# Moving one input load to another queue, and the output weights behind four small copies, in a fused Mamba-2 and bilinear FFN kernel

## The chip, the cores and the metric

The kernel runs on one core of one Trainium2 chip. The metric is device time in microseconds (us) of one execution, and of several executions the median. Engines are named as in the profile: PE (TensorE, matmuls; PEld is its weight load), DVE (VectorE), ACT (ScalarE), POOL (GpSimd) and SP (SyncE, which here only issues DMAs). ACT and POOL issue DMAs too.

## What is computed

The input is a state-space layer with decay, in chunks, followed by a bilinear feed-forward layer. x is (4, 8, 768, 32), a (4, 8, 768), B and C (4, 8, 768, 16); the weights w_a and w_b are 256 x 1536 and w_out is 1536 x 256. Cut to what matters:

```
cum = cumsum(log(a))                      # inside a chunk
M = (C @ B.T) * exp(cum_i - cum_j), j <= i
y = M @ x + exp(cum) * (C @ state)
state = exp(sum(log a)) * state + sum_j B_j x_j exp(cum_last - cum_j)
x2 = y, heads side by side                # (3072, 256)
out = ((x2 @ w_a) * (x2 @ w_b)) @ w_out   # (3072, 256), f32
```

The result does not depend on the chunk length. The kernel works with blocks of 128 tokens.

## The kernel before

**Tiling.** 768 tokens make six blocks of 128. Four batch elements make two pairs per block, so there are twelve "pairs": pairs 0 and 1 are block 0, pairs 2 and 3 block 1, and so on. For a block, products of decays (`scan`, L248, into `Pr`) are turned into factors per token. B is divided by them and C multiplied (`scale_bc`, L324, tiles `bm` and `cm` for pairs 0 and 1; `scale_q`, L341, into `planes` for later blocks), both are transposed, and PE forms scores C B^T (`scores`, L398) in four PSUM banks `SC`. `mask` (L442) multiplies the scores with a causal table, on DVE straight from PSUM or on POOL after an ACT copy. PE multiplies the masked scores with x (`pv_u`, `pv1`, `pv_b`), and the state is carried from block to block. The result, in f16, is the moving operand of the feed-forward matmuls: `unit_mm` and `bunit` multiply with `Wa` and `Wb`, ACT copies the first product out of PSUM, DVE multiplies it with the second, and `out_mm` or `bout` multiply with `Wo`.

**Order.** The order of the instructions on each engine is written out by hand in the program's body from L772 on; nothing reorders it. Each engine runs its own list in order and waits on semaphores for the others. Warm-up matmuls on constants (`warmup`, L236) stand between the first steps. PSUM banks of the feed-forward part come from a string, `BANKS`, one digit for each request of a bank (`bank`, L129); a new user of a bank waits for the last reader of it.

**Loads.** At the start SP and ACT request a, B and C of pairs 0 and 1 (L193 to L203); each pair's B or C comes in two halves by batch element, bt 0 and 1, of 64 KB. POOL requests x of pairs 0 and 1 (the first two DMAs of L228 to L234), and the weights, converted to f16 on the way: halves 0 of `Wa` and `Wb` between x of pair 0 and x of pair 1, then half 1 of `Wa`, and half 1 of `Wb` at L814. `Wo` comes in two halves by `load_wo` (L864 and L876). Block 1's C and B (`load_q` at L815, tiles `cq` and `bq`) are requested by SP, the first of them behind the landing of the first `Wa`, to which a dependency is written; x of block 1 in f32 and later B follow on SP.

```
pair 1:  scale_bc (cm, then bm) -> transposes -> bt, ct -> scores(1) -> mask x4 -> pv1 -> X2T -> unit_mm
block 1: mid_rows -> turned_rows -> batch_factors (FC) -> scale_q -> turn -> scores(2), scores(3)
```

`mid_rows(0, 1)` (L787) makes one block's rows of factors on POOL, `turned_rows` (L863) transposes them on DVE, and the four copies of `batch_factors` (L865) spread them to `FC` on POOL, where `scale_q` of block 1 reads them. `scan(4, 5)` (L808) prepares the decays of the fifth block and is needed by `over_mid(2, NBLK)` (L826).

Of the kernel before, what the change touches and what calls it, by code (L numbers as in the profile page):

```python
# [19 lines left out]
SS = 64.0  # L20

BANKS = (
    "012313213212312312031203123021032103120312013201320130231021302130231203120312013023102310"
    "2312013201320132012301230123012301230123012301320132013201320132013201320132013201320"
)


# [1 line left out]
def kernel(  # L29
# [13 lines left out]
    nc = tc.nc  # L43

    nb, H, S, D = x.shape
# [32 lines left out]
    Wa = [big.tile([128, 2, KC], f16, name=f"Wa{t}") for t in range(2)]  # L78
# [50 lines left out]
    def bank(name):  # L129
        return psf.tile([128, 512], f32, name=name, tag=f"ff{next(banks)}")  # L130
# [9 lines left out]
    def by_token(t_):  # L140
        return t_.rearrange("p h r n -> p (h r n)").rearrange("p (t h n) -> p t h n", t=2, h=H)

    def load1(eng, p, which, bt, i0=0, n=64, to=None):
        blk, bp = divmod(p, NBP)
        if p >= P2:
            return eng.dma_start(
                by_token(pair_in[p][which])[:, bt],
                (B, C, x)[which][2 * bp + bt, :, blk * Q : (blk + 1) * Q, :].rearrange("h q n -> q h n"),
            )
        src = (B, C, x)[which][2 * bp + bt, :, blk * Q + 2 * i0 : blk * Q + 2 * i0 + 2 * n, :]  # L150
        if to is None:
            to = pair_in[p][which]
        return eng.dma_start(
            to[64 * bt + i0 : 64 * bt + i0 + n].rearrange("i h r n -> i h (r n)"),
            src.rearrange("h (i r) n -> i h (r n)", r=2),
        )
# [3 lines left out]
    def load_q(eng, blk, parts=ALL_Q):  # L160
        if blk not in by_batch:
            by_batch[blk] = [inq.tile([128, H, 4, N], f32, name=n_, tag=n_) for n_ in ("bq", "cq")]
        return [
            eng.dma_start(
                by_batch[blk][w][32 * b : 32 * b + 32].rearrange("i h s n -> i h (s n)"),
                (B, C)[w][b, :, blk * Q : (blk + 1) * Q, :].rearrange("h (i s) n -> i h (s n)", s=4),
            )
            for w, b in parts
        ]
# [12 lines left out]
    def load_w(half, W):  # L182
        src = moe_w_a if W is Wa else moe_w_b
        c = slice(half * KC, (half + 1) * KC)
        return nc.gpsimd.dma_start(W[half], src.rearrange("(f p) e -> p f e", p=128)[:, :, c])

    def load_wo(half):
        return nc.gpsimd.dma_start(
            Wo[:, 6 * half : 6 * half + 6].rearrange("p (g kk) e -> p g (kk e)", kk=3),
            moe_w_out.rearrange("(g p kk) e -> p g (kk e)", p=128, kk=3)[:, 2 * half : 2 * half + 2],  # L190
        )
# [6 lines left out]
    load1(nc.scalar, 0, 1, 1)  # L198
    load1(nc.sync, 0, 1, 0, 0, 32)
    load1(nc.scalar, 0, 1, 0, 32, 32)  # L200
    for w in (1, 0):
        load1(nc.sync, 1, w, 0)
        load1(nc.scalar, 1, w, 1)  # L203
    nc.scalar.preload_act_table_set("natural_log_exp_and_others")
    nc.vector.memset(zero, 0.0)
    nc.gpsimd.memset(ident, 1.0)
# [21 lines left out]
    for p in range(2):  # L228
        for bt in range(2):
            load1(nc.gpsimd, p, 2, bt)  # L230
        if p == 0:
            w0 = load_w(0, Wa)
            load_w(0, Wb)
    load_w(1, Wa)  # L234

    def warmup(bank, *widths):  # L236
        for cols in widths:
# [10 lines left out]
    def scan(lo, hi):  # L248
        for k in range(lo, hi):
            nc.vector.tensor_tensor_scan(Pr[:, k], a_sb[:, k], zero, 1.0, ALU.mult, ALU.add)  # L250
# [4 lines left out]
    def sel_over_mid(lo, hi, eng):  # L255
        eng.tensor_tensor(
            out=selr[:, lo:hi].rearrange("p k t c -> p k (t c)"),
            in0=sel.rearrange("p t b h -> p (t b h)").unsqueeze(1).broadcast_to((BH, hi - lo, 2 * NBP * H)),
            in1=rmid[:, lo:hi].unsqueeze(2).broadcast_to((BH, hi - lo, 2 * NBP * H)),
            op=ALU.mult,  # L260
        )
# [24 lines left out]
    def mid_rows(lo, hi, eng):  # L286
        k = slice(lo + NBLK - NT, hi + NBLK - NT)
        eng.tensor_tensor(
            out=Ps[:, lo:hi], in0=Pr[:, k], in1=rmid[:, k].unsqueeze(2).broadcast_to((BH, hi - lo, Q)), op=ALU.mult
        )  # L290

    def clear(t_, eng):
        words = t_.rearrange("p c s -> p (c s)").bitcast(u32).rearrange("p (g w) -> p g w", g=3)
        eng.memset(words[:, 0:2, 32:96], 0)

    def turned_rows(lo, hi):
        nc.vector.transpose(
            Pt[:, lo:hi].rearrange("p k s c -> p (k s) c"), Ps[:, lo:hi].rearrange("p k (i s) -> p k s i", s=4)
        )

    def batch_factors(lo, hi, *bs, eng=None):
        for b in bs:
            (eng.tensor_copy if eng else nc.scalar.copy)(
                FC[32 * b : 32 * b + 32, lo:hi].rearrange("p k s h -> p (k s) h"),
                Pt[:, lo:hi].rearrange("p k s (b h) -> p (k s) b h", b=nb)[:, :, b],
            )
# [17 lines left out]
    def scale_bc(p, which, eng, factor=None):  # L324
        blk, bp = divmod(p, NBP)
        name, f = (("bm", fB), ("cm", fC))[which]
        if p >= P2:
            f = (fBl, fCl)[which][:, blk - P2 // NBP].rearrange("p (b t h) -> p b t h", b=NBP, t=2)[:, bp]
        else:
            f = f[:, blk, :, bp]  # L330
        raw = by_token(pair_in[p][which]) if p >= P2 else pair_in[p][which].rearrange("p h r n -> p r h n")
        m_ = mid.tile([128, 2, H, N], f16, name=name, tag=name)
        eng.tensor_tensor(
            out=m_,
            in0=raw,
            in1=(f if factor is None else factor).unsqueeze(3).broadcast_to((128, 2, H, N)),
            op=ALU.mult,
        )
        st.setdefault(p, {})[name] = m_
# [94 lines left out]
    def product0(m2, e):  # L434

        return (
            st[0]["T1"][:, 2 * m2 : 2 * m2 + 2].rearrange("p m (e r) q -> p e m (r q)", e=2)[:, e],
            (SC0, SC1)[m2][:, :, e * 256 : e * 256 + 256],
            causal.rearrange("p r q -> p (r q)").unsqueeze(1).broadcast_to((128, 2, 2 * Q)),
        )  # L440

    def mask(out_in, by_pool=False):  # L442
        o_, i_, c_ = out_in
        if by_pool:
            tmp = mid.tile([128, *c_.shape[1:]], f32, name="tmp", tag="tmp")
            nc.scalar.copy(tmp, i_)  # L446
            nc.gpsimd.tensor_tensor(out=o_, in0=tmp, in1=c_, op=ALU.mult)  # L447
        else:
            nc.vector.tensor_tensor(out=o_, in0=i_, in1=c_, op=ALU.mult)  # L449
# [110 lines left out]
    def evac0(u, bt, eng, py):  # L560
        o_, i_ = X2T[:, 0, bt, u], py[bt][:, u * Q : (u + 1) * Q]
        if eng is nc.scalar:
            nc.scalar.activation(out=o_, in_=i_, func=AF.Copy, scale=YS / SS)
        else:
            nc.vector.tensor_scalar(o_, i_, YS / SS, None, ALU.mult)
# [49 lines left out]
    def times(p, k2, b_ps, asb, by_pool=False):  # L615
        s = st[p]
        if "hk" not in s:
            s["hk"] = ffh.tile([128, NK, 2 * Q], f16, name="hk", tag="hk")
        eng = nc.vector
        if by_pool:  # L620
            eng, b_ps = nc.gpsimd, evac_a(b_ps)
        eng.tensor_tensor(  # L622
            out=s["hk"][:, 2 * k2 : 2 * k2 + 2, :].rearrange("p k q -> p (k q)"), in0=b_ps, in1=asb, op=ALU.mult
        )
# [159 lines left out]
    scale_bc(0, 1, nc.vector, v.rearrange("p (r b h) -> p r b h", r=2, b=NBP)[:, :, 0])  # L784
    over_mid(1, 2)
    sel_over_mid(1, 2, nc.vector)
    mid_rows(0, 1, nc.gpsimd)  # L787
    tb, tcp = bank("tb"), bank("tc")
    transposes(0, [tb, tcp], lambda: warmup(SC[3], 256))
    nc.scalar.copy(flat(fC, 0, 1), v)  # L790
# [3 lines left out]
    mask(product0(0, 0))  # L794
    mask(product0(0, 1))
    mask(product0(1, 1), by_pool=True)
    mask(product0(1, 0))
    clear(planes[0], nc.gpsimd)
    warmup(tcp, 512)
# [5 lines left out]
        evac0(0, bt, nc.scalar, py)  # L805
    warmup(tcp, 512, 128)
    scale_bc(1, 1, nc.vector)
    scan(4, 5)  # L808
    scale_bc(1, 0, nc.vector)
    clear(planes[1], nc.gpsimd)  # L810
    pv_u(0, 1, py, True)
    for bt in range(2):
        evac0(1, bt, (nc.scalar, nc.vector)[bt], py)
    load_w(1, Wb)  # L814
    for i_ in load_q(nc.sync, 1):  # L815
        tc.add_manual_dep(i_.ins, w0.ins.name, AFTER, reason="first weights ahead of block 1")
    for p in (2, 3):
# [43 lines left out]
    nc.scalar.copy(G.rearrange("p g k -> p (g k)"), gps)  # L861
    times(0, 2, bps[2], asb[2])
    turned_rows(0, 1)  # L863
    load_wo(0)  # L864
    batch_factors(0, 1, *range(nb), eng=nc.gpsimd)  # L865
    mid_rows(1, NT, nc.gpsimd)
    go((1, 0))
    batch_inverse(0, 1)
# [198 lines left out]
```

## Time and profile before

| | |
|---|---|
| median of 3 runs | 122.73 us (122.69 to 123.84) |
| profiled execution | 122.69 us |
| span of its instructions | 120.8 us |
| PE busy | 115.9 us (96% of the span) |
| DVE, ACT, POOL busy | 90.2, 67.9, 58.8 us |
| moved by DMA | 12.13 MB, mean 100 GB/s |

The time of an execution holds about 1.9 us more than the span. In the profile a row of the timeline gives start, duration, engine, line, operation, the tiles (out<-in), the shape and the count of merged instructions, and in brackets the idle time of the engine before it with what ended it. A busy PE is one that has work, not one at its peak. Rows of DMA requests give the tile, the engine that issues, the count, the size, and the time from request to landing; a request on POOL also occupies POOL, 0.6 to 0.9 us each here for the first twelve. Where two instructions of DVE follow one another, the second starts some 0.08 us before the first is written out. PE's matmul records overlap likewise, so that its pace is read from start to start.

### The profile page before, as it was taken

The page shows a single profiled execution, that of the slowest core. Times are in us where ns is not written, and L with a number is a line of the kernel's source. Part 1 is how long each engine was busy: PE and PEld are TensorE (multiplying, and loading weights), DVE is VectorE, ACT ScalarE, POOL GpSimd, SP SyncE. Part 2 cuts the span into 40 slices and gives each one's busy share as a digit, 9 for nine tenths or more (in the row PEclk, how much of TensorE's full clock was granted, in tenths as well). Part 3 has the DMA queues.
Part 4 walks back from the last instruction along what each step waited for, and adds up shares of the span by engine and source line. Part 5 has one row for each costly group of instructions (what it writes and reads, how often), then busy time and mean ns, then how long its engine had stood idle before and what let it go on. Part 6 is the DMA issues. An engine that isn't in the chain of part 4 may idle for free.

```text
span 120.8 us, 3551 instructions
## 1 busy us (share of the span) xinstructions
PE 115.9 (96%) x1385; PEld 73.9 (61%) x1386; DVE 90.2 (75%) x166; ACT 67.9 (56%) x136; POOL 58.8 (49%) x92
## 2 busy tenths in 40 slices
PE   7989999999999999999999999999999999999990
PEld 2436789888644488544485464775465684645880
DVE  5998988999798994599966999686899426758000
ACT  0446756769776646567666646635735637475230
POOL 7994986999699969387803994200000000000000
PEclk9999999999999999999999999999999999999999
DMA  3999999894789994959992929012001111010132
GB/s 63 135 183 192 207 230 197 134 200 113 99 94 161 115 139 101 110 68 121 218 241 89 85 9 121 5 46 87 5 6 40 43 49 44 0 43 0 43 108 71
DMA packets 59297, 12.13 MB, mean 100 GB/s; under 512 B 54480, under 2 KB 59216, under 8 KB 59280
## 3 DMA queue, kind: packets, MB, share of 16 engines
q0 software_dynamic: 20320, 3.80, 38.9%
q1 hardware_dynamic: 36432, 7.74, 34.8%
q10 hardware_dynamic: 2528, 0.36, 1.8%
q8 instruction: 11, 0.18, 0.7%
q14 instruction: 6, 0.05, 0.1%
HBM read 12.42 MB, written 3.15 MB: 129 GB/s over the span
## 4 chain that ended last, share of the span: by engine, by line
PE 92%; DVE 4%; issue 0%; ACT 0%
PE ops L693 22%; PE aps L667 22%; PE bps L667 21%; PE ops L637 5%; PE aps L598 4%; PE SC L404 4%; PE bps L598 3%; DVE t L449 3%; PE SC L238 3%; PE SC L473 2%; PE SC L536 1%; PE tc L238 1%; PE py L458 1%; PE SC L485 1%; DVE bt L385 1%
## 5 line engine op out<-in xcount | busy, mean ns | idle before, releaser
L612 ACT COPY asb<-aps 128x512 f32<-128x512 f32 x72 | 42.0, 587 | 17.2 <-PE aps L667 13.4
L679 DVE TENSOR_TENSOR hkb<-bps,asb 128x512 f16<-128x512 f32 x60 | 40.2, 687 | 12.7 <-ACT asb L612 11.1
L667 PE MATMUL aps<-XB,Wa 128*128 128x512 f16 x120 | 35.7, 379 | 0.0
L667 PE MATMUL bps<-XB,Wb 128*128 128x512 f16 x120 | 35.7, 379 | 0.0
L693 PE MATMUL ops<-Wo,hkb 128*128 128x256 f16 (+1 forms) x252 | 28.1, 268 | 0.0
L693 PEld LDWEIGHTS <-hkb 128*128 128x128 f16 x252 | 23.0, 98 | 3.8
L667 PEld LDWEIGHTS <-Wb 128*128 128x128 f16 x120 | 12.4, 103 | 13.6
L667 PEld LDWEIGHTS <-Wa 128*128 128x128 f16 x120 | 12.1, 103 | 11.7 <-issue 0.5
L449 DVE TENSOR_TENSOR t<-SC,causal_q 128x512 f16<-128x512 f32 x27 | 17.3, 681 | 2.4 <-PE SC L404 2.4
L705 ACT ACTIVATE osb<-ops 128x256 f32<-128x256 f32 (+1 forms) x20 | 7.6, 379 | 18.4 <-PE ops L693 18.4
L447 POOL TENSOR_TENSOR t<-tmp,causal_q 128x512 f16<-128x512 f32 x5 | 5.8, 1161 | 10.0 <-ACT tmp L446 10.0
L177 POOL DMA_DIRECT2D xn<-in_x_dram x8 | 9.5, 1192 | 0.0
L346 POOL TENSOR_TENSOR planes<-cq,FC 128x256 f16<-128x256 f32 x10 | 7.6, 775 | 2.2 <-DMA cq<-in_C_dram 2.1
L622 DVE TENSOR_TENSOR hk<-bps,asb 128x512 f16<-128x512 f32 x11 | 7.2, 672 | 0.9 <-ACT asb L612 0.8
L346 POOL TENSOR_TENSOR planes<-bq,FB 128x256 f16<-128x256 f32 x10 | 7.7, 772 | 0.4 <-DMA bq<-in_B_dram 0.4
L449 DVE TENSOR_TENSOR t<-SC,causal 128x512 f16<-128x512 f32 x11 | 7.0, 675 | 0.4 <-PE SC L404 0.3
L598 PE MATMUL aps<-X2T,Wa 128*128 128x256 f16 x48 | 6.8, 274 | 0.0
L446 ACT COPY tmp<-SC 128x512 f32<-128x512 f32 x10 | 5.9, 589 | 1.5 <-PE SC L404 1.1
L598 PE MATMUL bps<-X2T,Wb 128*128 128x256 f16 x48 | 6.6, 273 | 0.0
L558 ACT ACTIVATE XB<-SC 128x512 f16<-128x512 f32 (+1 forms) x9 | 4.6, 547 | 3.5 <-PE SC L501 2.4
L447 POOL TENSOR_TENSOR t<-tmp,causal 128x512 f16<-128x512 f32 x5 | 5.8, 1161 | 0.0
L637 PE MATMUL ops<-Wo,hk 128*128 128x256 f16 x48 | 5.8, 273 | 0.0
(101 smaller groups left out, 109.2 us busy)
## 6 DMA issues: line engine op xcount, KB each, us to landing
out_dram<-osb SPq DMA_DIRECT2D x23, 128.0 KB, 1.8
cq<-in_C_dram SPq DMA_DIRECT2D x20, 64.0 KB, 3.9
bq<-in_B_dram SPq DMA_DIRECT2D x18, 64.0 KB, 3.8
bn<-in_B_dram SPq DMA_DIRECT2D x8, 128.0 KB, 4.1
xn<-in_x_dram POOLq DMA_DIRECT2D x8, 128.0 KB, 5.9
Wa<-in_moe_w_a_dram POOLq DMA_DIRECT2D x2, 384.0 KB, 7.3
Wb<-in_moe_w_b_dram POOLq DMA_DIRECT2D x2, 384.0 KB, 7.9
Wo<-in_moe_w_out_dram POOLq DMA_DIRECT2D x2, 384.0 KB, 6.5
```

The source lines that it names most:

```text
L177: eng.dma_start(by_token(pair_in[p][which]).rearrange("p t h n -> p (t h) n"), src.rearrange("t h q n -> q (t h) n"))
L346: eng.tensor_tensor(out=plane[:, c0 : c0 + 4 * step].rearrange("p (j c) s -> p j s c", c=step)[:, :, :, 0:N], in0=by_batch[blk][which][:, ...
L447: nc.gpsimd.tensor_tensor(out=o_, in0=tmp, in1=c_, op=ALU.mult)
L449: nc.vector.tensor_tensor(out=o_, in0=i_, in1=c_, op=ALU.mult)
L598: nc.tensor.matmul(ps[:, kk * 2 * Q : (kk + 1) * 2 * Q], W[k // 6][:, f, k % 6 // 3 * 384 : (k % 6 // 3 + 1) * 384].rearrange("p (c kk) -> ...
L612: (nc.vector.tensor_copy if on_dve else nc.scalar.copy)(asb, a_ps)
L622: eng.tensor_tensor(out=s["hk"][:, 2 * k2 : 2 * k2 + 2, :].rearrange("p k q -> p (k q)"), in0=b_ps, in1=asb, op=ALU.mult)
L637: nc.tensor.matmul(o_ps[:, 0:d_model], hk[:, k, bt * Q : (bt + 1) * Q], Wo[:, k, :], start=(k == 0), stop=(k == NK - 1), skip_group_check= ...
L667: nc.tensor.matmul(t_, W[k // 6][:, f, k % 6 // 3 * 384 : (k % 6 // 3 + 1) * 384].rearrange("p (c kk) -> p kk c", kk=3)[:, k % 3], XB[:, b ...
L679: return lambda: nc.vector.tensor_tensor(out=s["hk"][:, k], in0=ps[1], in1=asb, op=ALU.mult)
L693: nc.tensor.matmul(o_ps[:, 0:w], hk[:, k, c * Q : (c + 1) * Q], Wo[:, k, cs], start=(k == 0), stop=(k == NK - 1), skip_group_check=True,)
L705: nc.scalar.activation(out=o_sb[:, 0:w], in_=o_ps[:, 0:w], func=AF.Copy, scale=1.0 / (YS * YS))
```

## The change

Pair 1's B of bt 1 is requested by POOL, right behind x of pair 0 and ahead of the first weights, instead of by ACT. On ACT the request of pair 1's C of bt 1 is cut into two of half the rows. Half 1 of `Wa` is requested behind POOL's mask of pair 0 instead of with the first loads. `mid_rows(0, 1)` moves from ahead of that mask to behind the request of half 1 of `Wb`. `scan(4, 5)` moves from between `cm` and `bm` of pair 1 to behind the copies of pair 0's output. The first half of `Wo` is requested behind the four copies of `batch_factors` instead of ahead of them. The string of PSUM banks is another one: except for the seventh and eighth entry, each entry follows the same earlier user of its bank as before.

```diff
-    "012313213212312312031203123021032103120312013201320130231021302130231203120312013023102310"
-    "2312013201320132012301230123012301230123012301320132013201320132013201320132013201320"
+    "012313123121321321032103213012031203210321023102310230132012301230132103210321023013201320"
+    "1321023102310231021302130213021302130213021302310231023102310231023102310231023102310"
...
-    for w in (1, 0):
-        load1(nc.sync, 1, w, 0)
-        load1(nc.scalar, 1, w, 1)
+    load1(nc.sync, 1, 1, 0)
+    load1(nc.scalar, 1, 1, 1, 0, 32)
+    load1(nc.scalar, 1, 1, 1, 32, 32)
+    load1(nc.sync, 1, 0, 0)
...
         if p == 0:
+            load1(nc.gpsimd, 1, 0, 1)
             w0 = load_w(0, Wa)
             load_w(0, Wb)
-    load_w(1, Wa)
...
     sel_over_mid(1, 2, nc.vector)
-    mid_rows(0, 1, nc.gpsimd)
     tb, tcp = bank("tb"), bank("tc")
...
     mask(product0(1, 1), by_pool=True)
+    load_w(1, Wa)
     mask(product0(1, 0))
...
     scale_bc(1, 1, nc.vector)
-    scan(4, 5)
     scale_bc(1, 0, nc.vector)
     clear(planes[1], nc.gpsimd)
     pv_u(0, 1, py, True)
     for bt in range(2):
         evac0(1, bt, (nc.scalar, nc.vector)[bt], py)
+    scan(4, 5)
     load_w(1, Wb)
+    mid_rows(0, 1, nc.gpsimd)
...
     turned_rows(0, 1)
+    batch_factors(0, 1, *range(nb), eng=nc.gpsimd)
     load_wo(0)
-    batch_factors(0, 1, *range(nb), eng=nc.gpsimd)
     mid_rows(1, NT, nc.gpsimd)
```

## The prediction

> **What bounds the kernel now.** I read the page's busy shares and slices first, then the chain, then the rows in order of time for the first 26 us, and last the DMA requests one at a time.
>
> ```profile
> PE   7989999999999999999999999999999999999990
> PEclk9999999999999999999999999999999999999999
> ...
> PE 92%; DVE 4%; issue 0%; ACT 0%
> ```
>
> TensorE is busy in nearly every slice at the full granted clock and carries 92% of the chain. Apart from ACT's last copy at 117.6, the chain's pieces on other engines all lie before 13.9 us. From 14.85 us the matmuls follow one another, so a gain or a loss has to come from the first 14 us or from a new wait later. Around pair 1's entry the rows read:
>
> ```profile
> 8.99 0.46 DVE L333 TENSOR_TENSOR cm<-cn,fC 128x256 f16<-128x256 f32 x1
> 9.37 0.41 DVE L250 TENSOR_TENSOR_SCAN Pr<-a_sb,zero 32x128 f32<-32x128 f32 x1
> 9.61 0.61 PE L238 MATMUL tc<-const-bfloat16-1.0 128*128 128x512 bf16 x2
> 9.70 0.39 DVE L333 TENSOR_TENSOR bm<-bn,fB 128x256 f16<-128x256 f32 x1
> 10.14 0.29 PE L374 MATMUL SC<-ident,bm 128*128 128x128 f16 x2
> 10.32 0.81 PEld L598 LDWEIGHTS <-Wa 128*128 128x128 f16 x8
> 10.58 0.69 DVE L385 TENSOR_TENSOR bt<-SC,par 128x512 f16<-128x512 f16 x1 [0.29 <-PE SC L374]
> ```
>
> VectorE scales C (cm), scans, then scales B (bm), end to start without a gap; PE's transposes (L374) start 0.06 us after bm ends at 10.08. The DMA answers for one request each (copied in order of request):
>
> ```profile
> xn<-in_x_dram POOLq DMA_DIRECT2D x1, 64.0 KB, 3.9
> bn<-in_B_dram ACTq DMA_DIRECT2D x1, 64.0 KB, 6.0
> Wa<-in_moe_w_a_dram POOLq DMA_DIRECT2D x1, 384.0 KB, 5.8
> Wb<-in_moe_w_b_dram POOLq DMA_DIRECT2D x1, 384.0 KB, 7.0
> cq<-in_C_dram SPq DMA_DIRECT2D x1, 64.0 KB, 7.9
> Wo<-in_moe_w_out_dram POOLq DMA_DIRECT2D x1, 384.0 KB, 6.9
> ```
>
> The last column is us from request to landing. They were requested at 3.38 (x), 3.60 (pair 1's B, second batch), 4.06 (first Wa), 4.76 (first Wb), 11.23 (last of block 1's C) and 15.11 (first Wo). So that B lands at 9.6: the scan fills a wait for it. Wa lands at 9.8 to 9.9 and is first used at 10.32; Wb at 11.8, used at 12.05; that C at 19.2, where GpSimd has waited 1.4 us for it; Wo at 22.0, used at 23.89. Margins are 0.4, 0.25, none and 1.9 us.
>
> ```profile
> 19.32 1.37 POOL L346 TENSOR_TENSOR planes<-cq,FC 128x256 f16<-128x256 f32 x2 [1.38 <-DMA cq<-in_C_dram]
> 20.54 0.77 POOL L346 TENSOR_TENSOR planes<-bq,FB 128x256 f16<-128x256 f32 x1
> 21.34 0.58 DVE L359 STREAM_TRANSPOSE turned<-planes 128x384 f32<-128x384 f32 x1
> ...
> 25.40 0.65 PE L404 MATMUL SC<-turned 32*64 32x128 f16 x32
> ```
>
> This is the second place where a load reaches PE: C, GpSimd's scaling, the turn at 21.34 (0.03 after GpSimd ends at 21.31), and VectorE's row of products and masks, which ends at 25.35 just before scores L404.
>
> **The change, part by part.** The profiled execution took 122.69 us, 120.8 of span and 1.9 around it; the median of the three runs is 122.73, so the two sums differ by 0.04.
>
> *B through GpSimd, the scan behind.* ACT still issues five requests (0.65 each; one C in halves, one B gone): nothing, and the table load at 4.28 stays. The halves of C go out at 2.94 and 3.60; even with the 6.0 of the old B the later one lands at 9.6, and with the 3.9 of the C before it at 7.5, against a use at 8.99. I take 7.5, since the weights that the old B trickled in among now start later. Their cost is 0, at most 0.6. On GpSimd B is requested at 4.06 and everything behind it moves back by one issue, 0.72. B's landing is bounded by 3.9 (x, the same size directly ahead on the same queue), giving 8.0, and 6.0, giving 10.1. I take 8.0. With B there and the scan gone, bm runs 9.37 to 9.75, 0.33 earlier. But PE's two filler matmuls (9.61, 0.226 from start to start) free PE only at 10.06: the transposes gain 0.08, not 0.33. Then bt 10.50, scores, masks and pair 1's product keep the 0.08; the scan runs at 9.95 to 10.35 between the copy of X2T and bt, while PE transposes. Gain 0.08; the bounds are 0.08 (fillers) and a loss of 0.4.
>
> *Weights behind B.* Each of the first two is requested 0.72 later. If landing moves with the request, Wa comes at 10.55 (0.3 late against a use now at 10.24) and Wb at 12.5 (0.5 late). If it goes by bytes, nothing moves: the windows view gives a DMA share of 1.04 to 1.74 (packets overlap) in each 2 us from 3 to 21 us, B's 64 KB only change place, and q0 carried 107% of sixteen engines' time between 7.0 and 9.2 while B's 144 remaining packets on q10 took 8.7%. I take 0 (the engines, not the request, limit it); ends 0 and +0.5.
>
> *Second Wa and Wb, row products, clears.* GpSimd's mask waits for ACT's copy, done at 7.76, and then runs 7.80 to 8.95 (was 8.01 to 9.16); second Wa is issued at 8.95, both clears, second Wb at 10.05 (was 9.40), mid_rows 10.8 to 11.2. GpSimd's next work is hr at 11.87, before which it idled 1.49, so this hides; without that cover it would cost 0.4. Nobody needs mid_rows' result before 15.31. The earlier mask gives nothing: pair 0's second product waits for ACT's copy of the same bank (ended 9.33). Second Wb landed at 18.1 and is used at 19.16; 0.65 later leaves 0.4. Second Wa landed at 15.75, used at 18.1.
>
> *Wo behind the four factor copies.* The copies wait for Pt, ready at 15.71, so they start 0.1 sooner (15.75 to 16.7), Wo is issued at 16.7 instead of 15.11, and mid_rows(1, ..) ends at 18.5 instead of 17.94, before DVE's use at 18.95. Wo's landing is bounded by 22.0 (all bytes ahead of it are the same) and 16.7 + 8.9 = 25.6 (the longest landing of a weight load, second Wa). I take 16.7 + 6.1 = 22.8 (second Wo's), before its use at 23.7: cost 0, end +1.9. What it frees: from 17.5 to 19.5 the queues show q0 (Wo) with 90% of the engines and q1 with 30%, and exactly then the last C and B of block 1 were landing. With Wo's packets 1.6 later I take those loads 0.3 to 0.8 sooner, so GpSimd starts at 18.6 to 19.0 and the turn is released by VectorE itself. Scores L404 at 25.40 come 0.312 after the matmul start before them; the other scores (11.34, 21.98) show 0.202. That 0.11 was a wait for VectorE's masks and goes. Ends 0 and 0.11; I take 0.11. Where nothing frees, scores at 21.98 are held by the turn (ends 21.92) and the 0.08 from the start is lost there too.
>
> *Bank string.* Of 175 entries only the seventh and eighth follow another user: the second product of pair 0 takes the bank that VectorE's X2T copy frees, which the first already waits for. Cost 0.
>
> Sum: 122.69 - 0.08 - 0.11 = 122.50.
>
> **Two rules beside rows.** Row: B on ACT's queue took 6.0 us, x on GpSimd's 3.9. The Trainium skill, "DMA: Bandwidth & Descriptors", section "Issuing engines are not separate DMA queues", says that all requests share sixteen engines and that a second issuer saves only issue time; by that B would come no sooner and the sum would be 122.7, the first rival. The trace agrees on the shared engines; the rows differ by what stands ahead in each queue.
>
> Row: GpSimd's first eight requests took 0.69 to 0.87 us each, beside a busy VectorE. The Trainium skill, "SBUF — State Buffer", section "SBUF: two separate sides", warns that a GpSimd DMA's descriptors wait while VectorE holds a shared port, and "Who interferes with whom" advises the hardware path instead; that speaks against this move. Its section "A bandwidth-pool intuition that's wrong (but worth ruling out)" puts such a request at about 3.1 us instead of 0.62; with B's request alone that long, an estimate, the sum would be some 125. Nothing in these rows shows it.
>
> **Rivals.**
> 1. *Gains are lost downstream*: B lands later than 9.7, or block 1's loads do not come sooner and the turn holds the scores at 21.98. For it: the turn ends only 0.06 before them. Against: Wo leaves 17.5 to 19.5 free. Time 122.69 - 0 = 122.7.
> 2. *First weights late (slower)*: Wa and Wb land with their requests. For it: Wb's margin is 0.25 against a shift of 0.72. Against: the busy engines. It decides once Wb lands after 11.97; SP's loads of block 1, which wait for the first Wa (9.85 after 9.83), follow. Time 122.69 + 0.5 = 123.2, less if only part of the shift shows.
> 3. *A later weight is late*: Wo after 23.7 or second Wb after 19.08. For it: second Wb took 8.7. Against: margins of 0.9 and 0.4 by my landings. Time 122.5 + 0.2 to 1.9, middle 123.0; only its far end passes 1%.
> 4. *Requests on GpSimd stretch* beside VectorE, pushing all weights back by a whole issue or more (2 x 0.72 past Wb's margin): 122.69 + 1.2 = 123.9 and up. Against: the even issue rows.
>
> **How the numbers follow.** Forecast 0.5, rival 1 0.22, rival 2 0.13, rival 3 0.12, rival 4 0.03. The likeliest is 122.5. Below it, the 0.33 by which bm comes earlier bounds what the start could give if the fillers yield: 122.3; I set 122.2. Above, 123.2 takes in rival 2 and the middle of rival 3. About 1% (1.2 us) is what a measurement of this kernel tells from no change. Faster by more asks for more than both gains together: 0.06. Slower by more is the end of rival 3 and rival 4: 0.08. Within: 0.86. The forecast's own range is 122.3 to 122.65.
>
> **What would show it.** B landing near 8.0, bm at 9.37, transposes at about 10.06, scores of pair 1 at 11.26: first step right. First Wa by 10.2 and Wb by 11.95, with no gap ahead of L598: second. GpSimd's planes at 18.6 to 19.0 and a start-to-start of 0.20 at the scores near 25.2: third. Wo landed before 23.7. A PE gap before L598 at 10.3 or 12, before 19.2, or before L637 at 23.8 would make the prediction wrong.

## The result, and the profile after

The changed kernel takes 123.45 us (median of 22 executions, 122.45 to 124.01), the kernel before 122.74 (22 executions, 122.43 to 123.84): the ratio is 1.0043, with a 95% interval of 1.0025 to 1.0061. By the ratio it is slower by some 0.5 us, by the medians by 0.7. That lies within the 1% called no change, but above the forecast of 122.50 and above the range around it, which ends at 123.2.

The profiled execution of the changed kernel is its fastest, 122.45 us, 0.05 from the forecast. It shows nearly every step as forecast. That it meets the forecast is luck, and it is a poor witness for the median, one us higher. So it is read first, and then two other profiled executions of the same kernel. Page of the changed kernel, slices and chain:

```profile
PE   7999999999999999999999999999999999999990
...
PE 92%; DVE 4%; issue 0%; ACT 0%
```

TensorE carries the chain as before. Rows of its timeline around pair 1's entry, VectorE's first, then TensorE's (lines lie one further than before):

```profile
9.04 0.41 DVE L334 TENSOR_TENSOR cm<-cn,fC 128x256 f16<-128x256 f32 x1
9.37 0.42 DVE L334 TENSOR_TENSOR bm<-bn,fB 128x256 f16<-128x256 f32 x1
10.11 0.40 DVE L251 TENSOR_TENSOR_SCAN Pr<-a_sb,zero 32x128 f32<-32x128 f32 x1
9.66 0.61 PE L239 MATMUL tc<-const-bfloat16-1.0 128*128 128x512 bf16 x2
10.11 0.27 PE L375 MATMUL SC<-ident,bm 128*128 128x128 f16 x2
10.33 1.04 PE L599 MATMUL aps<-X2T,Wa 128*128 128x256 f16 x8
12.11 0.93 PE L599 MATMUL bps<-X2T,Wb 128*128 128x256 f16 x7
```

`bm` starts at 9.37 as forecast, the scan stands behind, the transposes follow the two fillers at 10.11 (forecast 10.06; cm already starts 0.05 later in this execution). No idle time stands before L599, neither at `aps` nor at `bps`. One DMA request per row, last column us from request to landing, in order of request at 4.06, 4.74, 5.44 and 16.59:

```profile
bn<-in_B_dram POOLq DMA_DIRECT2D x1, 64.0 KB, 4.3
Wa<-in_moe_w_a_dram POOLq DMA_DIRECT2D x1, 384.0 KB, 5.2
Wb<-in_moe_w_b_dram POOLq DMA_DIRECT2D x1, 384.0 KB, 6.5
Wo<-in_moe_w_out_dram POOLq DMA_DIRECT2D x1, 384.0 KB, 5.8
```

B lands at 8.33 (was 9.63), Wa at 9.95, Wb at 11.98 and Wo at 22.4. Block 1, the same view's rows of POOL, DVE and PE:

```profile
19.07 1.37 POOL L347 TENSOR_TENSOR planes<-cq,FC 128x256 f16<-128x256 f32 x2 [0.60 <-DMA cq<-in_C_dram]
21.13 0.57 DVE L360 STREAM_TRANSPOSE turned<-planes 128x384 f32<-128x384 f32 x1
21.93 0.65 PE L405 MATMUL SC<-turned 32*64 32x128 f16 x32
25.24 0.65 PE L405 MATMUL SC<-turned 32*64 32x128 f16 x32
```

C is scaled 0.25 earlier than before, and the scores at 25.24 come 0.16 earlier. From the first product of block 1 (31.17) to the end of the span it is 89.5 us, as in the kernel before and in the two executions shown next. So all of the difference between these spans has to arise in the first 31 us.

Now the same kernel, profiled again at 123.20 us (run a1). The chain in order of time, start and us:

```profile
4.06 0.67 POOL bn L153
4.73 6.37 DMA Wa<-in_moe_w_a_dram
11.10 0.05 issue
11.15 1.05 PE aps L599 x8
```

and the rows of TensorE at that place:

```profile
10.17 0.27 PE L375 MATMUL SC<-ident,bm 128*128 128x128 f16 x2
11.15 1.05 PE L599 MATMUL aps<-X2T,Wa 128*128 128x256 f16 x8 [0.60 <-DMA Wa<-in_moe_w_a_dram]
```

Here the chain goes through one load. Wa, asked for at 4.73, lands at 11.10. The transposes are as early as before (10.17), but L599 starts at 11.15, 0.82 after the matmul ahead of it. That is the wait which was forecast not to come. In a third profiled execution (run d2, 123.16 us) Wa lands at 10.34 and L599 starts at 10.46, but time is lost at the turn:

```profile
21.07 0.77 POOL L347 TENSOR_TENSOR planes<-bq,FB 128x256 f16<-128x256 f32 x1 [0.26 <-DVE hk L623]
21.88 0.58 DVE L360 STREAM_TRANSPOSE turned<-planes 128x384 f32<-128x384 f32 x1 [0.54 <-POOL planes L347]
22.52 0.65 PE L405 MATMUL SC<-turned 32*64 32x128 f16 x32 [0.38 <-DVE turned L360]
25.94 0.65 PE L405 MATMUL SC<-turned 32*64 32x128 f16 x32
```

The last B of block 1 landed at 20.86 (19.82 on record), POOL scales it at 21.07, DVE turns it at 21.88 and the scores wait 0.38 in front of it. The bracket at POOL names VectorE, but its wait is taken for the load's: in five profiles (before, d2, a4, e2, e3) POOL starts 0.21 behind this landing. The request of that B goes back to the first Wa as well: SP makes the eight requests of block 1 one after the other, the first at 10.36, 0.02 behind Wa's landing.

**Two doors.** In all seventeen profiles used here, the experiments' too, the second scores of block 1 (near 25 us) start within 0.05 of the later of (first product `aps` + 14.91) and (turn + 4.06), and in all but one the first product of block 1 is 5.92 to 5.95 behind them (6.29 in a3). With the trace's times in us:

| profiled execution | us | Wa landed | transposes | `aps` | last B of block 1 | turn | scores |
|---|---|---|---|---|---|---|---|
| before, on record | 122.69 | 9.83 | 10.14 | 10.38 | 20.33 | 21.34 | 25.40 |
| before (d1) | 122.85 | 10.58 | 10.24 | 10.62 | 20.43 | 21.45 | 25.56 |
| change, on record | 122.45 | 9.95 | 10.11 | 10.33 | 19.82 | 21.13 | 25.24 |
| change (a1) | 123.20 | 11.10 | 10.17 | 11.15 | 20.26 | 21.98 | 26.09 |
| change (d2) | 123.16 | 10.34 | 10.24 | 10.46 | 20.86 | 21.88 | 25.94 |
| change, Wo first (a4) | 123.24 | 11.05 | 10.08 | 11.10 | 21.05 | 22.07 | 26.12 |
| change, B on ACT (a2) | 122.89 | 10.18 | 10.59 | 10.82 | 20.43 | 21.63 | 25.74 |
| same, weights 0.66 later (e3) | 122.69 | 10.55 | 10.06 | 10.60 | 20.46 | 21.48 | 25.54 |

The first door opens at the later of transposes + 0.22 and Wa + 0.05. The change brings the transposes forward and lets Wa come later.

### The profile page after: what moved, and what is told of

It reads as the page before. It is cut to its first block, busy times and chain, and to the rows that moved or that the text cites. A ratio compares the mean times of both kernels' runs of the same rounds, so it can differ in the third digit from the quotient of the medians.

```text
span 120.7 us, 3553 instructions
## 1 busy us (share of the span) xinstructions
PE 115.9 (96%) x1386; PEld 73.8 (61%) x1386; DVE 90.1 (75%) x166; ACT 67.9 (56%) x136; POOL 59.5 (49%) x93
## 4 chain that ended last, share of the span: by engine, by line
PE 92%; DVE 4%; issue 0%; ACT 0%
PE ops L694 22%; PE aps L668 22%; PE bps L668 21%; PE ops L638 5%; PE aps L599 4%; PE SC L405 4%; PE bps L599 3%; DVE t L450 3%; PE SC L239 3%; PE SC L474 2%; PE SC L537 1%; PE tc L239 1%; PE py L459 1%; PE SC L486 1%; PE fps L272 1%; DVE bt L386 1%
## 5 line engine op out<-in xcount | busy, mean ns | idle before, releaser
L599 PE MATMUL aps<-X2T,Wa 128*128 128x256 f16 x48 | 6.8, 274 | 0.0
L599 PE MATMUL bps<-X2T,Wb 128*128 128x256 f16 x48 | 6.6, 273 | 0.0
```

The source lines that it names most:

```text
L599: nc.tensor.matmul(ps[:, kk * 2 * Q : (kk + 1) * 2 * Q], W[k // 6][:, f, k % 6 // 3 * 384 : (k % 6 // 3 + 1) * 384].rearrange("p (c kk) -> ...
```

## The experiments

The theories: **T1**, the first weights land late because B stands ahead of them in POOL's queue (T1a: since they are requested 0.68 later; T1b: since B's bytes and descriptors pass first). **T2**, the later place of second Wa or of Wo disturbs block 1's loads. **T3**, no cause at all: the 1.0043 is scatter between executions. Ratios are to the kernel before on the same chip, with 95% intervals; runs with one first letter shared a chip. The medians of the kernel before were 122.97 (a), 123.13 (c), 123.02 (d) and 123.11 us (e).

### Again, and one part undone

**a1**, the change unedited.

> The changed kernel once more, nothing edited, for a second profile and more times. Theory T1 (the first weights lose their margin): in the profile of the change the first Wb landed at 11.98 us where PE wants it at about 12.0, so in most executions it, or the first Wa, lands later and PE shows a gap ahead of L599 near 10.3 or 12.1 us, of 0.5 to 1.2 us where the time is 123.3 to 123.9; the ratio is again 1.003 to 1.006. Theory T2 (a later weight is late): no gap before 15 us, but one of that size ahead of the second halves' first use near 18 or 19 us or ahead of the output matmuls near 23.8 us. Theory T3 (the executions merely scatter): the ratio is within 0.998 to 1.002.

Measured 123.44 us, 1.0038 [1.0008, 1.0069]. The loss is there a second time; the profile is the one shown above.

**a2**, the change with pair 1's loads requested as before; all the rest of the change stays.

```diff
-    load1(nc.sync, 1, 1, 0)
-    load1(nc.scalar, 1, 1, 1, 0, 32)
-    load1(nc.scalar, 1, 1, 1, 32, 32)
-    load1(nc.sync, 1, 0, 0)
+    for w in (1, 0):
+        load1(nc.sync, 1, w, 0)
+        load1(nc.scalar, 1, w, 1)
...
-            load1(nc.gpsimd, 1, 0, 1)
```

> The change with pair 1's loads as before: B of bt 1 again requested by ACT as the last of its five, C of bt 1 whole, first weights one request earlier; all else as changed. T1: the first weights have their margin again, 122.5 to 122.8, ratio to the kernel before 0.998 to 1.001. T2: no help, ratio 1.003 to 1.006. T3: 0.998 to 1.002 like the others.

Measured 123.18 us, 1.0009 [0.9981, 1.0036]. The loss is not seen, but the interval overlaps a1's; e3 and e4 add to it below. The edit also takes back the halving of C's request on ACT, which no run changes by itself; in d3 the loss is there with C whole. The rows show what is paid instead (the last is a DMA request):

```profile
10.11 0.42 DVE L332 TENSOR_TENSOR bm<-bn,fB 128x256 f16<-128x256 f32 x1 [0.47 <-DMA bn<-in_B_dram]
10.82 1.04 PE L597 MATMUL aps<-X2T,Wa 128*128 128x256 f16 x8
bn<-in_B_dram ACTq DMA_DIRECT2D x1, 64.0 KB, 6.5
```

B, requested at 3.59 on ACT, lands at 10.08 and `bm` waits 0.47 for it: this is the wait that the change removes. Wa (10.18) is ready before it is needed.

**a3**, the change with second Wa requested with the first loads, as in the kernel before.

```diff
             load_w(0, Wb)
+    load_w(1, Wa)
...
-    load_w(1, Wa)
     mask(product0(1, 0))
```

> The change with the second half of Wa requested with the first loads again, behind x of pair 1; all else as changed. T1: the first weights are as late as in the change, ratio 1.003 to 1.006. T2, if the second half of Wa or what queues behind it is the late one: ratio 0.998 to 1.001. T3: 0.998 to 1.002.

Measured 123.02 us, 1.0012 [0.9978, 1.0045], which decides nothing. Its profile, at 124.46 us far above its median, shows Wa at 11.37 and x of pair 1 at 15.5: the first Wa is late with second Wa in its old place too.

**a4**, the change with Wo ahead of the four copies again.

```diff
+    load_wo(0)
     batch_factors(0, 1, *range(nb), eng=nc.gpsimd)
-    load_wo(0)
```

> The change with the first half of Wo requested ahead of the four factor copies again; all else as changed. T1: no help, ratio 1.003 to 1.006. T2, if Wo is the late one: ratio 0.998 to 1.001. T3: 0.998 to 1.002. Block 1's last B should land some 0.3 to 0.5 us later than in the change (19.8), and the wait of 0.11 us ahead of the scores near 25.3 us comes back if it hangs on that.

Measured 123.46 us, 1.0039 [1.0013, 1.0066], the same loss as a1's. Wo's place neither costs nor brings anything that shows. T2 falls for Wo. For second Wa and Wb a2 speaks: it requests them as late as the change does, and its last B of block 1 lands at 20.43, as in the kernel before.

### How much of B, and how the weights stand behind it

**c1**, the change with 16 of B's 64 rows through POOL and 48 through ACT.

```diff
-    load1(nc.scalar, 1, 1, 1, 0, 32)
-    load1(nc.scalar, 1, 1, 1, 32, 32)
+    load1(nc.scalar, 1, 1, 1)
+    load1(nc.scalar, 1, 0, 1, 16, 48)
...
-            load1(nc.gpsimd, 1, 0, 1)
+            load1(nc.gpsimd, 1, 0, 1, 0, 16)
```

> The change, but GpSimd's extra request carries only 16 of the 64 rows of pair 1's B (16 KB); ACT requests the other 48 in B's old place, C whole. The first weights are requested as late as in the change. T1a (the later request of the weights makes them land late): the first Wa lands near 11 us as in three of four profiles of the change and its variants, ratio 1.003 to 1.006. T1b (the 64 KB of B in the same ring ahead of the weights do it): Wa lands by 10.3, as in the two profiles with B on ACT (9.8 and 10.2), ratio 0.999 to 1.002.

Measured 123.20 us, 0.9987 [0.9964, 1.001], Wa at 10.02. By itself that spoke for bytes (T1b), though its median lies above that of the kernel before.

**c2**, the kernel before with the loads moved and nothing else of the change.

```diff
-    for w in (1, 0):
-        load1(nc.sync, 1, w, 0)
-        load1(nc.scalar, 1, w, 1)
+    load1(nc.sync, 1, 1, 0)
+    load1(nc.scalar, 1, 1, 1, 0, 32)
+    load1(nc.scalar, 1, 1, 1, 32, 32)
+    load1(nc.sync, 1, 0, 0)
...
         if p == 0:
+            load1(nc.gpsimd, 1, 0, 1)
             w0 = load_w(0, Wa)
```

> The kernel before, with the move of pair 1's B and the halves of C alone. T1a and T1b: the whole of the loss is here, first Wa near 11 us, a gap of 0.5 to 1 us ahead of the first Wa product near 10.3 us, ratio 1.003 to 1.006. T2 (a later weight): 0.999 to 1.001.

Measured 123.35 us, 1.0018 [0.9997, 1.0039], which neither shows the expected loss nor excludes it. Rows of POOL, DVE and PE:

```profile
7.49 0.77 POOL L185 DMA_DIRECT2D Wa<-in_moe_w_a_dram  x1
8.32 0.39 POOL L290 TENSOR_TENSOR Ps<-Pr,rmid 32x128 f32<-32x128 f32 x1
8.69 1.14 POOL L449 TENSOR_TENSOR t<-tmp,causal 128x512 f16<-128x512 f32 x1
9.13 0.99 DVE L335 TENSOR_TENSOR cm<-cn,fC 128x256 f16<-128x256 f32 x1
10.37 0.39 DVE L335 TENSOR_TENSOR bm<-bn,fB 128x256 f16<-128x256 f32 x1
10.81 0.28 PE L376 MATMUL SC<-ident,bm 128*128 128x128 f16 x2
```

With second Wa and mid_rows still ahead of it, POOL's mask moves back by the extra request (8.69, it was 8.01) and ends at 9.83. VectorE's cm, 0.46 long in the kernel before, takes 0.99 here and ends 0.29 behind the mask. The scan and `bm` follow it, and the transposes start at 10.81, behind `bm`: B's early landing (8.09) is worth nothing. The other moves of the change put second Wa and mid_rows behind the mask and so clear the way. Wa lands at 10.72, within 0.15 of the kernel before (d1), so this kernel says little of T1.

**c3**, the change with both of pair 1's B halves through POOL, 128 KB ahead of the weights.

```diff
-    load1(nc.sync, 1, 0, 0)
...
+            load1(nc.gpsimd, 1, 0, 0)
             load1(nc.gpsimd, 1, 0, 1)
```

> The change, with the other half of pair 1's B moved from SP to GpSimd too, ahead of the first weights: twice the suspected bytes and requests. T1a: the weights are requested another 0.7 us later, Wa lands near 11.7, time 0.6 over the change, ratio 1.008 to 1.011. T1b: 64 KB more in the ring, 0.3 us at 200 GB/s, ratio 1.005 to 1.009. T2: as the change, 1.003 to 1.006.

Measured 123.11 us, 0.9986 [0.9967, 1.0004]: no slower than before, though twice the bytes stand ahead of the weights and T1a and T1b both expected 1.005 or more. Wa, requested at 5.40, lands at 10.71. But after the first product of block 1 this kernel needs 89.06 us and not 89.5, for a reason that has nothing to do with B's bytes (last part of the experiments). Without that 0.43 (0.35%) the ratio would be 1.0021.

**c4**, the change with the first Wa requested in two halves of its columns.

```diff
-    def load_w(half, W):
+    def load_w(half, W, lo=0, hi=KC):
...
-        c = slice(half * KC, (half + 1) * KC)
-        return nc.gpsimd.dma_start(W[half], src.rearrange("(f p) e -> p f e", p=128)[:, :, c])
+        c = slice(half * KC + lo, half * KC + hi)
+        return nc.gpsimd.dma_start(W[half][:, :, lo:hi], src.rearrange("(f p) e -> p f e", p=128)[:, :, c])
...
-            w0 = load_w(0, Wa)
+            load_w(0, Wa, 0, 384)
+            w0 = load_w(0, Wa, 384, 768)
```

> The change, with the first half of Wa requested in two pieces of 384 columns; the first product needs only the first piece. T1: the first product starts near 10.3 again and the second, 0.44 later, waits for the second piece; the time falls by 0.2 to 0.45 from the change, ratio 1.000 to 1.003. If the slowest of the sixteen engines is late in either piece the fall is at the low end, and the extra request may cost the first Wb 0.1 to 0.3. T2: no change, 1.003 to 1.006.

Measured 123.99 us, 1.0074 [1.0047, 1.0102]: worse, where 1.000 to 1.003 was expected. The first piece lands at 9.19 and `aps` starts at 10.44, 0.22 behind the transposes; then

```profile
10.44 1.04 PE L600 MATMUL aps<-X2T,Wa 128*128 128x256 f16 x8
13.00 0.51 PE L600 MATMUL bps<-X2T,Wb 128*128 128x256 f16 x3 [0.61 <-DMA Wb<-in_moe_w_b_dram]
```

Wb, asked for one request later, lands at 12.96 and L600 stands for it. A wait taken from one load was handed to the next in the queue. In this execution (123.48 us, half a us under the median) not even that wait sets the time: the last C of block 1 lands at 20.10 and its last B at 20.99, the turn starts at 22.27 and the scores at 26.33, 4.06 behind it, where the first door with the wait of 0.61 would have opened at about 26.0.

### The same again on another chip

**d1**, the kernel before; **d2**, the change; **d3**, c1 again; **d4**, c3 again; each unedited.

> The kernel before, unedited, for a second profile of it. Ratio 0.998 to 1.002. T1 says that its B of bt 1 lands between 9.6 and 10.2 us (9.63 in its first profile, 10.08 in the variant with B on ACT) and its first Wa by 10.3, so that either sets pair 1's entry and its time lies near 122.7 to 123.2.

> The change, unedited, a third profile, on the same chip as the others of this call. T1: B lands near 8.5 and the first Wa near 11.0 (11.10 and 9.95 so far), ratio 1.003 to 1.006. T3 (scatter of executions and chips): 0.998 to 1.002.

> A quarter of B on GpSimd, the rest on ACT, again, beside the change on one chip. If the bytes of B in the weights' ring are what delays Wa (T1b): Wa by 10.3, ratio 0.997 to 1.001, below the change by 0.3 to 0.6 us. If the request 0.5 later is enough (T1a): Wa near 11, as the change.

> Both halves of B on GpSimd ahead of the weights, again, beside the change on one chip. T1a and T1b both put it above the change by 0.3 to 0.6 us. Its first run said 0.9986 on another chip, with Wa landing at 10.71 in the profile; if it is again below the change, neither the bytes nor the request ahead of Wa explain the change's loss, but which queues are left busy beside the weights' own: with both halves gone from SP and ACT nothing small is left to trickle in among the weights.

Measured: d1 122.99 us, 0.9996 [0.9977, 1.0015]; d2 123.42, 1.0043 [1.0018, 1.0068]; d3 123.48, 1.0044 [1.0024, 1.0064]; d4 123.23, 1.0008 [0.9985, 1.0031]. A second copy of the kernel before comes out even, the change comes out 0.4% slower for the third time: T3 falls for the change. The sliver is as slow as the change this time, with Wa at 10.93; what c1 seemed to say on bytes does not stand. Both halves are even again, and with the 0.35% taken out 1.0043. c1 and d3 are the same kernel, and their intervals (up to 1.001, from 1.0024) do not even meet: from one call to the next a ratio moves by more than its interval says, and by as much as the effect sought. So a single ratio decides little here, and e3's below, too, stands on one call.

### The delay without the bytes, and the end of the program

**e3**, a2 with a POOL instruction ahead of the first Wa that clears part of a tile cleared later anyhow, so that Wa is requested at 4.71 and no B passes there.

```diff
         if p == 0:
+            nc.gpsimd.memset(planes[2][:, 0:172], 0.0)
             w0 = load_w(0, Wa)
```

**e4**, a2 again beside it.

> The change with B on ACT as before, and GpSimd kept busy for 0.7 us (a fill of a buffer that is not yet in use) ahead of the first weights: the later request of the weights without a byte more in their ring. T1a (the request time): first Wa between 10.7 and 11.4, ratio 1.003 to 1.006. T1b (B's bytes in the ring): Wa as in the next kernel, 9.8 to 10.6, ratio within 0.002 of it.

> The change with pair 1's loads as before, once more, as the partner of the kernel with the delay. Ratio 0.999 to 1.002; B lands at 9.6 to 10.1 and sets pair 1's transposes, Wa lands at 9.8 to 10.6.

Measured: e3 122.92 us, 0.9989 [0.9969, 1.0009]; e4 123.20, 1.0011 [0.9997, 1.0025]. (e4's profiled execution, at 125.18 us, is far above its median and left out of the table and of the means; B landed at 11.06 in it, later than expected.) The request of Wa in e3, and the rows of Wa and of ACT's B:

```profile
4.71 0.71 POOL L185 DMA_DIRECT2D Wa<-in_moe_w_a_dram  x1
```

```profile
Wa<-in_moe_w_a_dram POOLq DMA_DIRECT2D x1, 384.0 KB, 5.8
bn<-in_B_dram ACTq DMA_DIRECT2D x1, 64.0 KB, 4.7
```

The delay costs nothing that shows: 0.9989 with it, 1.0009 and 1.0011 without. Wa does come 0.37 later than a2's (10.55 for 10.18), but ACT's B lands at 8.24 instead of 10.08. From 8.0 to 10.1 us ACT's queue still moves 84 packets in a2 and none in e3: with the weights asked for later, B no longer trails in among them. In c1 and d3, where the weights are asked for 0.5 later, the 48 rows on ACT land at 8.19 and 7.97 too. T1a falls as a cause of the loss, as far as one call shows it, and B's early landing, which the change wanted from another queue, is had here by a delay alone.

**e1** and **e2**, the kernel before and the change, with one store of the fifth block issued by POOL.

```diff
-                (nc.sync, nc.scalar)[part].dma_start(rows[:, cs], o_sb[:, 0:w])
+                eng = nc.gpsimd if (blk, c) == (4, 0) else (nc.sync, nc.scalar)[part]
+                eng.dma_start(rows[:, cs], o_sb[:, 0:w])
```

> The kernel before with one output store of block 4 issued by GpSimd instead of SP, 15 us ahead of the end. SP and ACT take turns through eight completion semaphores; at the end SP waits for them in a fixed order, and in the kernel before the last store holds the first place, so that the seven others are walked after it has landed (1.35 us from its landing to the end; 0.92 in the two profiles with both halves of B on GpSimd, which have one such DMA less). One store less on SP puts the last store in the last place: 0.43 us less, ratio 0.996 to 0.997. If the 0.43 came from something else in those kernels: 0.999 to 1.001.

> The same store moved in the changed kernel: 0.43 us below the change, whose ratio was 1.0043, so 1.000 to 1.002; it also counts as one more profile of the change up to block 4, with the first Wa between 10.0 and 11.1 us.

Measured: e1 122.34 us (122.25 to 122.54, 6 executions), 0.9943 [0.993, 0.9956]; e2 122.97, 0.9995 [0.997, 1.0019]. e1 beats both kernels. The waits of SP's queue in the last stretch (line, releaser, us in total, times, longest), of the kernel before:

```profile
SPq L1062 <- DMA out_dram<-osb: 1.8, 1, 1.8
SPq L1062 <- PEq L1062: 0.7, 2, 0.5
```

and of e1:

```profile
SPq L1063 <- DMA out_dram<-osb: 1.2, 3, 0.5
SPq L1063 <- PEq L1063: 0.7, 2, 0.5
```

At the end SP waits for the completion semaphores of all queues in a fixed order, some 0.064 us each. The DMAs of SP and ACT take eight semaphores in turn. In the kernel before, the last store holds the one that is waited for first, so that seven more waits come after it: 1.35 us from the last landing to the end. With one store less in the turn the last store holds the one that is waited for last: 0.92 us. (The change itself keeps the number, 89: it takes B from ACT and cuts C in two.) That 0.43 shows in the rest of the span behind block 1's first product, 89.52 before, 89.06 (e1), 89.07 (e2), 89.06 and 89.05 (c3 and d4, where a load less does the same). e1's median gained 0.77, so that 0.3 of it is not accounted for, with six executions behind it. What e1 and e2 have between them is still the change, some 0.5%, on the chip on which e3 and e4 lose nothing that shows.

## Why the prediction was wrong, by its own steps

- *B through GpSimd, the scan behind*: right. B landed at 8.21 to 8.68 in the change's profiles (forecast 8.0, bounds 8.0 and 10.1), and the transposes stood at 10.11 to 10.24 (forecast 10.06). It was under-valued, if anything: in the trace of before B came nearly in time, and with B on ACT it lands as late as 10.2 and holds the transposes to 10.6 and 10.7 (a2, e1). The Trainium skill, "DMA: Bandwidth & Descriptors", section "Issuing engines are not separate DMA queues", has a second issuer save only issue time; here B came 1.3 us sooner from another queue, while requested 0.46 later. What counted was its place ahead of the weights and not the queue as such: e3 has B as early on ACT's.
- *Weights behind B*: this step failed. It said "I take 0 (the engines, not the request, limit it); ends 0 and +0.5". The 0 held on record (9.95 against 9.83): Wa landed at 11.10 and 10.34 in the two other unedited profiles, 11.05 in a4. Over eleven profiles with some B in POOL's queue (c4's cut Wa left out) the mean is 10.70 (9.95 to 11.37), over five without 10.30 (9.83 to 10.58). That is 0.4 for the 0, with scatter as large, so that the size is not firm; the ratios carry the sign. The upper end was too low as well: a1 lies 1.3 above the trace of before, twice the shift of the request. What misled was one row of one execution: 9.83 was early for the kernel before too (d1: 10.58), and the margin of 0.4 read from it was luck. Rival 2 named the place and the price (123.2; the median is 123.45), with a chance of 0.13. Its reason, landing with the request, is not the one: e3 delays the request alone and costs nothing that shows.
- *Second Wa and Wb, row products, clears*: hidden, as forecast; c2 shows what they would cost left in place (transposes at 10.81). Of what hangs on POOL's mask (7.96 to 9.12, forecast 7.80 to 8.95) the prediction looks at pair 0's product alone; VectorE's cm hangs on it too.
- *Wo behind the copies*: its own landing was right (22.2 to 22.4 in the three unedited profiles; forecast 22.8, use 23.8 or later), rival 3 did not come. The gain failed, the second step that did: block 1's last B was to land 0.3 to 0.8 sooner and did so on record alone (0.5); in a1 it was 0.07 sooner and in d2 0.53 later. Over twelve profiles with B in POOL's queue the mean is 20.87, over five without 20.35. A part is the same lateness again, since SP asks for these loads only when the first Wa is there (first request at 11.12 in a1, 9.97 on record).
- *The 0.11 at the scores*: right in kind. It is the second door's excess over the first, and it is gone where the turn is early enough (change on record, a1) and back where it is not (d2).
- *Requests stretched on GpSimd* (rival 4), *bank string*: neither seen. POOL's first ten requests of the change took 0.69 to 0.87 us each, as in the kernel before.

In sum, where -0.19 us was forecast, some +0.5 came. It is shown as far as this: the loss comes with B's move into POOL's queue (1.0043, 1.0038 and 1.0043 with it, 1.0009, 0.9989 and 1.0011 with the change but for it and the halving of C). It enters by the first weights: in the chains by Wa, at `aps` or by way of SP's requests for block 1, once by Wb (c3), and the later request alone does not make it. Not settled is how B's 64 KB do it. In the windows view, from 7 to 9 us, all queues together move

```profile
7.00:9.00 2.00, 1.63 (x36) 0.84 (x29) 1.82 (x4) 0.70 (x2) 1.94 (x3) 1.00 1.16 192
```

in the kernel before (last column GB/s; ahead of it the DMA share) and

```profile
7.00:9.00 2.00, 1.89 (x60) 0.88 (x45) 1.61 (x3) 0.59 (x1) 1.93 (x3) 1.00 0.91 101
```

with both halves ahead (d4). It is 163 to 192 GB/s in five profiles without B in POOL's queue, 146 to 183 in eight with the 64 KB, 101 in two with 128 KB. There the DMA share falls much less than the GB/s (0.91 for 1.16), so that B's small packets (128 B each) do take the engines' time; for 64 KB the ranges overlap. Wa's landing can be taken apart further. Its semaphore is counted up in sixteen steps, read here as one for each DMA engine; the load has landed with the last. From the traces, in us:

| profiles | eighth step | last step |
|---|---|---|
| no B in POOL's queue (before, d1, e1, a2) | 9.37 to 9.54 | 9.83 to 10.58 |
| the delay alone (e3) | 9.76 | 10.55 |
| 16 KB (c1, d3) | 9.60, 9.54 | 10.02, 10.93 |
| 64 KB (record, a1, a3, a4, c2, d2, e2) | 9.49 to 9.88 | 9.95 to 11.37 |
| 128 KB (c3, d4) | 10.22 | 10.66, 10.71 |

With 128 KB, where Wa is also asked for 1.3 later, the bulk of it moves by 0.7. With 64 KB the bulk comes no later than with the delay alone (mean 9.65), and what spreads is the end: the last step lies 0.5 to 1.0 behind the eighth in the five profiles without B there, 0.5 to 1.8 with the 64 KB. In a1 eleven steps are done by 9.85 and the last five come from 10.29 to 11.10. Single packets of the weights (1,536 B) took up to 1.05 us there against a median of 0.135, but as long in e3. Why the last engines are late, and whether they are so more often behind B, no run here shows.

## What to carry to other kernels

A load has landed when the last of its sixteen steps has come, and one profile is one draw of that: a margin of 0.4 us under a load of 5 to 6 us was no margin, so profile the kernel before twice before a load's slack is spent. Moving a load ahead of others in a queue pays only if every load behind it has slack; look at what waits for these, and for what hangs on their landing in other queues. Where a load is needed early, it can be enough to start the bulk a little later (e3, which had B early without the loss, though without a gain in time that shows) rather than to move the load into the bulk's queue. And a ratio of some tenths of a per cent has to come out a second time before it is believed (c1 and d3).

## What the runs showed of the hardware that was not expected

- A 384 KB load, requested at the same time to 0.02 us in the same kernel, landed from 9.95 to 11.10 (change), and 9.83 to 10.58 (kernel before). The last of sixteen steps make the difference: fifteen were done by 9.61 in the kernel before, eleven by 9.85 in a1.
- The time from the last store's landing to the end depends on which of eight semaphores that store drew: 1.35 to 1.36 us in the fourteen profiles of kernels with 89 DMAs on SP and ACT, 0.91 to 0.92 in the four with 88 (c3, d4, e1, e2). It is nearly as large as the whole effect of this change, and a comparison of kernels with different counts of DMAs is off by it.
- VectorE's cm, which multiplies two tiles, did not get done beside POOL's mask, which does so too. In five profiles (a3, c2, c3, c4, d4) cm started 0.3 to 0.7 us before the end of the mask; there it took 0.59 to 0.99 us and ended 0.27 to 0.29 behind the mask. In the others it started at most 0.17 before that end and took 0.41 to 0.46.
- The Trainium skill, "DMA: Bandwidth & Descriptors", section "Queues, rings and completion order", says that each engine goes round its rings by packets of several descriptors. That would let a ring of small descriptors fall behind a ring of large ones, as B did on ACT's queue (10.08 in a2; 8.24 in e3, where the weights start 0.66 later); the runs agree with it and do not prove it.
